# A recurrent attention and gated feed-forward kernel: the decay row on ScalarE's queue, more idle products in front, and a new order of emission

## The chip, the cores and the metric

The kernel runs on one core of one Trainium2 chip. The metric is the device time of one execution in microseconds (us), lower is better. The engines are named TensorE (PE, its weight loads PEld), VectorE (DVE), ScalarE (ACT), GpSimd (POOL) and SyncE (SP); an engine's instruction queue for DMA issues is written SPq or ACTq.

## The reference

An attention with a decaying state runs over 768 steps for 4 batches and 8 heads of width 48; its output feeds a layer with 3072 rows, 384 inputs and 2048 hidden units.

```python
def _attn_ref(r, k, v, w, u):
    state = np.zeros((B, H, D, D), dtype=np.float32)
    for t in range(S):
        kt, vt, rt = (k[:, :, t], v[:, :, t], r[:, :, t])
        cur = np.einsum('bhd,bhe->bhde', u[None] * kt, vt)
        y[:, :, t] = np.einsum('bhd,bhde->bhe', rt, state + cur)
        state = w[None, :, :, None] * state + np.einsum('bhd,bhe->bhde', kt, vt)

def _moe_ref(x, w_in, w_out):
    h = x @ w_in
    sp = np.where(h > 20.0, h, np.log1p(np.exp(np.minimum(h, 20.0))))
    return ((h * np.tanh(sp)) @ w_out).astype(np.float32)
```

## The kernel before

**Tiling.** The 768 steps are cut into 6 chunks of 128; a chunk and a batch make one attention step `s` (24 of them, `NS`). Four steps make one group of 512 rows, which then goes through the feed-forward layer in 16 tiles of hidden units (`up`: `hp` is a PSUM bank; `down`: three accumulators `acc0` to `acc2`). Each attention step has these pieces, each a small generator: `dots` (a product `q` of r and k on VectorE, and matrix products of it with `us`, two columns wide for the first two steps, whose sums `sd` ScalarE copies out), `scale` (multiplies r and k by powers of the decay, `TR`), `diag` (spreads `sd` over the diagonal of `P`), `keys` (multiplies k by the table `TKn`), `attend` (scores into `pa` or `pb`, and a predicated copy into `P`), `outputs` (rows of y into `yt` and `hp`, and the state), `finish` (copies y into `x`). Around them stand `convert` (weights arrive as 64-bit words and are turned to floats: one pass on ScalarE, three on VectorE), `split` (a weight into a high and a low part), and for each pair of tiles `evacuate` (copies `hp` to `hb`) and `gate` (two table loads, three functions on ScalarE, and on VectorE the product `gf` for the first tiles or `hb`, `gh` and `gl` for later ones).

**The first steps.** A prologue builds the powers of the decay from the decay row `wt`, a 2 KB transfer that SyncE issues ahead of everything else; VectorE's chain of L310 to L324 depends on it. SyncE then issues the list `FIRST` in order: `rk`, weight blocks (`raw`), `v`, `rkn`. ScalarE issues `cst`, the constants (mask, unit, `us`). `token_table` builds `TKn` from the decay powers: ScalarE spreads (L340), TensorE multiplies into `pb`, ScalarE copies (L351).

**Idle products.** `keep_warm` issues matrix products of zeros, which nothing reads. `WARM0` of them stand at the very front (three write into `pa` and `yt`, the rest into `idle`). Later, where the planner sees TensorE free for longer than `WARM_MIN`, it inserts `int(gap / FILL)` more; this ends with the first tile of the feed-forward layer.

```python
            if e == "pe" and self.fill and t - self.free[e] > WARM_MIN:
                begun = self.begun
                self.fill(t - self.free[e] - LAT)
...
    flow.fill = lambda us: keep_warm(int(us / FILL))
```

**The order.** The instructions of all engines are emitted in an order that a planner (`Flow`) computes when the kernel is built. It walks through the pieces, each a generator that yields what it waits for and what it costs on which engine, and picks at each turn the piece whose engine is free first, with a rank to break near ties. `RANK`, `CONVERT` and `SHIFT` move single pieces in rank; `FREE` tells when each engine is free at the start, `LAND0` and `LAND` when the first transfers land. `REST` is the order of the transfers after `FIRST`, issued one weight block at a time. On the chip each engine executes its own instructions in this order and waits on semaphores.

Of the kernel before, what the change touches and what calls it, by code (L numbers as in the profile page):

```python
# [76 lines left out]
def first_use(c):  # L77
    return UNITS.index((0, c) if c < AHEAD else (None, WG * c))
# [4 lines left out]
    ("rk", 3), ("v", 3), ("rkn", 1), ("rkn", 3), ("rkn", 0),  # L83
)
REST = (
    ("raw", 2), ("raw", 3), ("raw", 4), ("rk", 4), ("rkn", 4), ("v", 4), ("un", 0), ("raw", 6), ("raw", 5),
    ("raw", 7), ("raw", 8), ("raw", 9), ("raw", 10), ("raw", 12), ("raw", 13), ("raw", 11), ("raw", 14),
    ("raw", 15),
)
LAND0, LAND = 3.15, dict(rk=1.32, v=0.66, raw=1.96, rkn=0.5, un=0.78)  # L90
ISSUE, QUEUED, LANDING, USE, BACKLOG = 0.5, 0.95, 1.9, 0.6, 4.2
GATE = dict(raw3=1, raw4=2)
HT = 2 * C
# [2 lines left out]
BY_STEP = 0  # L96
FROM, FROM2 = 8, 14
X_SPLIT = 3
CONVERT = (-984.856, -938.676, -1001.12, -999.777)
LAG = 6  # L100
WHOLE = 0
AHEAD_LEAST, AHEAD_MOST, DOWN = 2, 8, 1
LO0, HI0, LO1, HI1 = 0.0, 0.7, 0.1, 0.9
LAT, LAT0 = 0.15, 0.13
WARM0, WARM_MIN, FILL = 10, 0.3, 0.28
DMA_LAT = 2.5
BLOCK0, BLOCK, ASK, HELD, FETCH = 445, 256, 0.7, 2.9, 2.5
PATIENCE = dict(dve=0.1, act=0.1, pe=0.3)
URGENT = 8
RANK = dict(token_table=-900.2, keys=-899.9, first_state=-899.5)  # L110

COST = dict(dve=1.0)
FREE = dict(pe=5.6, act=2.8, dve=1.0, pool=1.7, sp=1.0, landed=1.0)

L_ATT, L_V, L_IN, L_OUT, L_GATE, L_EVAC, L_PUT, L_FIN = 2, 2, 9, 9, 3, 1, 12, 4


SHIFT = dict(
    attend4=-8, attend6=8, attend7=3, convert10=30, convert15=-30, convert3=30, convert4=-30, convert7=1,
    convert8=-30, convert9=1, diag10=1, diag3=100, dots12=-1, dots6=100, dots8=30, evacuate12=-30, evacuate22=-30,  # L120
    evacuate6=-3, evacuate8=-3, gate0=-8, gate12=30, gate2=1, gate5=3, gate8=-30, keys11=3, keys3=-3, keys6=30,
    outputs5=-8, outputs6=1.742, outputs8=-8, outputs9=-8, scale11=-3, scale8=0.8, split1=8, split10=-30, split12=3,
    split9=-30,
)


# [128 lines left out]
def rwkv_mish_kernel(ctx, tc, rkT, rkN, vN, wT, w_in, w_out, consts, rkF, vF, wF, uF, outT):  # L255
    nc = tc.nc
# [9 lines left out]
    un = const.tile([128, DM], F32, name="un")  # L266
# [3 lines left out]
    wt, w64, iw = (small[:, 4 + n * NP : 4 + (n + 1) * NP] for n in range(3))  # L270
    flags = small[:, 4 + 3 * NP : 4 + 3 * NP + N_FLAGS]
    more = small[:, 4 + 3 * NP + N_FLAGS :]
    zeros = const.tile([128, 1], F32, name="zeros")
    nc.vector.memset(zeros, 0.0)
    nc.scalar.dma_start(cst, consts[:, : N_CST + 2 * NP])
    mask = cst[:, :CK].bitcast(U32)
    unit = cst[:, CK:N_CST].bitcast(BF16)
# [15 lines left out]
    order.enter_context(tc.manual_schedule(engines={ET.SP, ET.PE, ET.DVE, ET.Pool, ET.Activation}))  # L293
    loaded, loads = {}, {}
    sync = mybir.DependencyInfo(mybir.DependencyClass.Sync, mybir.DependencyReason.DATA)
    nc.sync.dma_start(wt, wT)


    powers = const.tile([128, NP, CK + 1], F32, name="TR")
# [5 lines left out]
    def prologue():  # L305

        yield "wt"
        v, M = nc.vector, CK // 2
        yield {"dve": 1.75}
        v.tensor_scalar(out=wc, in0=wt, scalar1=W_LO, scalar2=W_HI, op0=ALU.max, op1=ALU.min)  # L310
        n = 1
        while n < M:
            new, old = (powers[:, :, M + 1 + a : M + 1 + a + n] for a in (n, 0))
            v.tensor_tensor(
                out=new, in0=old, in1=powers[:, :, M + n : M + n + 1].broadcast_to([128, NP, n]), op=ALU.mult
            )
            n *= 2
        v.reciprocal(out=iw, in_=w32)
        v.tensor_tensor(
            out=powers[:, :, :M], in0=powers[:, :, M : 2 * M], in1=iw.unsqueeze(2).broadcast_to([128, NP, M]), op=ALU.mult  # L320
        )
        flow.set("TRK")
        yield {"dve": 0.1}
        v.tensor_tensor(out=w64, in0=w32, in1=w32, op=ALU.mult)  # L324
        flow.set("w64")
# [8 lines left out]
    def token_table():  # L334
        yield "w64"
        for par in range(2):
            r = ROWS[par]
            yield {"act": 0.65}
            for p in range(NP):
                nc.scalar.activation(dw[r, p, par], unit[r, : CK - 1 - D : -1], AF.Copy, scale=w64[r, p : p + 1])  # L340
        yield "x1"
        yield pe(0.9, 32)
        t = pb[1]
        for p in range(NP):
            for half in range(2):
                matmul(
                    t[HALVES[half], 2 * p * D : 2 * (p + 1) * D], lhsT=TR[:112, p],
                    rhs=dw[:112, p].rearrange("d q e -> d (q e)"), start=True, stop=True,
                )
        yield act(384)  # L350
        nc.scalar.copy(out=TKn, in_=t[:, :DM])  # L351
        flow.set("TKn")
# [39 lines left out]

    flow = Flow(FREE, 2 * WARM0)
    flow.events["wt"] = 2.6
# [283 lines left out]
    def keys(s):  # L678
        yield f"rkn{s}"
        yield f"sd{s}"  # L680
        yield "TKn"
        yield dve(384)
        k = loaded[s][1][:, :DM]
        nc.vector.tensor_tensor(out=k, in0=k, in1=TKn, op=ALU.mult)
        flow.set(f"keys{s}")
# [141 lines left out]
    def outputs(s):  # L827
# [32 lines left out]
        if not rows:  # L860
            flow.start(first_state(s), s + RANK["first_state"], name=f"first_state{s}")
        elif not last:
# [42 lines left out]
    def first_state(s):  # L905
        yield "out1"
        yield f"keys{s}"
        if s:
            yield f"state{s - 1}"
        yield pe(0.5, 64)  # L910
        state_products(s, new_first, True)
        for b in range(2):
            engine = yield {**act(192), **dve(192)}
            (nc.scalar.copy if engine == "act" else nc.vector.tensor_copy)(
                out=states[r112, 2 * s + b, :, :D], in_=new_first[b][r112]
            )
        flow.set(f"state{s}")
# [477 lines left out]
    for s in range(NS):  # L1395
        if s < 2:
            flow.start(spread_v(s), rank(s) + 0.0045, 0.0, f"spread_v{s}")
        for k, thread in enumerate((load_step, load_v, scale, dots, diag, keys, attend, outputs)):
            if thread is keys and s >= NS - 2 or s <= B and thread in (load_step, load_v):
                continue  # L1400
            if thread is keys and s < B:
                flow.start(keys(s), s + (RANK["keys"] if s < 2 else -899.8), 0.0, f"keys{s}")
                continue
# [6 lines left out]
    flow.start(prologue(), -1100, 0.0, "prologue")  # L1410
    flow.start(token_table(), RANK["token_table"], 0.0, "token_table")
    for c in range(len(W_ORDER)):
        i, f = W_ORDER[c]
        at = first_use(f) + (LAG - L_OUT if i else -L_IN) + c / 1000
        flow.start(convert(c), CONVERT[c] if c < len(CONVERT) else at, 0.0, f"convert{c}")
    for n, (i, f) in enumerate(S_ORDER):
# [13 lines left out]
    with tc.If(in_range < 128 * N_FLAGS):  # L1430
# [48 lines left out]
        with tc.tile_pool(name="any2", bufs=1) as work:  # L1479
            raw = work.tile([128, WE, 2], U32, name="raw")  # L1480
# [117 lines left out]
```

## Time and profile before

| | |
|---|---|
| median of 3 runs | 481.77 us (481.13 to 482.31) |
| span of the profiled execution | 479.8 us (its own time is not stated apart from the span) |
| PE busy | 469.6 us, 98% |
| DVE busy | 375.8 us, 78% |
| ACT busy | 385.7 us, 80% |
| DMA | 60.17 MB, mean 125 GB/s |

The busy time of TensorE counts idle products and products at a low clock as well. The shares of VectorE and ScalarE are means over the whole span; the first quarter and the rest differ.

### The profile page before, as it was taken

The numbers are of one execution on the slowest core, as the hardware profiler recorded it, in microseconds if no ns is written. First come the engines' busy times: TensorE is split into PE (matmuls) and PEld (weight loads), VectorE is DVE, ScalarE is ACT, GpSimd is POOL, SyncE is SP. The second block draws the span as 40 slices with busy tenths as digits, with TensorE's granted clock in tenths as the row PEclk, the third lists the DMA queues.
The fourth block names the chain that finished last, engine by engine and source line by source line (L and its number), as shares of the span: only waits on it lengthen the run. The fifth ranks groups of instructions, "written<-read, shape, count | busy, mean of one in ns | idle before, by whom it ended". The sixth has DMA issues, their size and how long they took to land.

```text
span 479.8 us, 11503 instructions
## 1 busy us (share of the span) xinstructions
PE 469.6 (98%) x4918; PEld 381.5 (80%) x4918; DVE 375.8 (78%) x599; ACT 385.7 (80%) x488; POOL 4.6 (1%) x31
## 2 busy tenths in 40 slices
PE   8989999999999999999999999999999999999995
PEld 5778988657887888888888888888888888888883
DVE  7997999998999794889875789987788745555650
ACT  5669799899989887667879877888569798989961
POOL 1000000000000000000000000000000000000000
PEclk8999999999999999999999999999999999999999
DMA  7866676430424210245132446143463220221002
GB/s 311 293 232 214 222 279 207 153 101 10 162 85 133 79 38 0 102 156 188 66 120 67 165 146 219 62 133 104 165 210 107 66 83 28 105 81 51 1 0 73
DMA packets 20171, 60.17 MB, mean 125 GB/s; under 512 B 3312, under 2 KB 4304, under 8 KB 20112
## 3 DMA queue, kind: packets, MB, share of 16 engines
q1 hardware_dynamic: 17664, 55.11, 34.1%
q10 hardware_dynamic: 2448, 4.25, 2.5%
q8 instruction: 40, 0.66, 0.6%
q14 instruction: 19, 0.16, 0.1%
HBM read 52.57 MB, written 4.72 MB: 119 GB/s over the span
## 4 chain that ended last, share of the span: by engine, by line
PE 90%; DVE 5%; ACT 2%; DMA 1%; issue 1%; ACTq 0%; SPq 0%
PE hp L358 41%; PE acc L358 41%; PE pa L358 4%; PE yt L358 2%; DVE w L499 1%; PE idle L358 1%; DMA rk<-in_rkT_dram 1%; DVE rk L606 1%; PE pb L358 1%; DVE gl L1054 1%; DVE hb L1046 1%; DVE hb L1222 0%; ACT w L497 0%; ACT L1036 0%; ACT L1030 0%
## 5 line engine op out<-in xcount | busy, mean ns | idle before, releaser
L358 PE MATMUL hp<-x,w 128*128 128x512 f32 x720 | 172.7, 392 | 0.9 <-DVE hb L1222 0.9
L358 PE MATMUL acc<-gh,w 128*128 128x512 f32 x492 | 158.5, 391 | 0.0
L358 PEld LDWEIGHTS hp<-x,w 128*128 128x128 f32 x720 | 134.2, 188 | 29.6 <-DVE hb L1222 1.0
L358 PEld LDWEIGHTS acc<-gh,w 128*128 128x128 f32 x492 | 92.3, 188 | 19.4
L358 PE MATMUL acc<-gl,w 128*128 128x512 f32 x246 | 95.1, 389 | 0.0
L1046 DVE TENSOR_TENSOR hb<-hb,fa 128x1024 f32<-128x1024 f32 x40 | 48.8, 1219 | 37.4 <-ACT fa L1036 37.3
L1030 ACT ACT_TABLE_LOAD x48 | 61.6, 1283 | 13.3 <-DVE hb L1046 9.8
L1036 ACT ACT_TABLE_LOAD x47 | 60.3, 1283 | 0.8
L1222 DVE COPY hb<-hp 128x512 f32<-128x512 f32 x63 | 43.2, 686 | 19.5 <-PE hp L358 19.2
L1030 ACT ACTIVATE fa<-hb,small 128x1024 f32<-128x1024 f32 x48 | 55.4, 1153 | 2.6 <-DVE hb L1046 2.1
L358 PEld LDWEIGHTS acc<-gl,w 128*128 128x128 f32 x246 | 46.2, 188 | 9.5
L1033 ACT ACTIVATE fa<-fa 128x1024 f32<-128x1024 f32 x48 | 50.9, 1059 | 0.8
L1036 ACT ACTIVATE fa<-fa 128x1024 f32<-128x1024 f32 x47 | 49.8, 1060 | 0.5
L1054 DVE TENSOR_TENSOR gl<-hb,gh 128x1024 fp32r<-128x1024 f32 x40 | 48.8, 1220 | 0.8 <-ACT gh L1050 0.2
L358 PE MATMUL acc<-gf,wraw 128*128 128x256 f32 (+1 forms) x132 | 37.7, 439 | 1.2 <-issue 1.2
L358 PEld LDWEIGHTS acc<-gf,wraw 128*128 128x128 f32 x132 | 25.6, 196 | 10.9 <-issue 8.6
L1222 ACT COPY hb<-hp 128x512 f32<-128x512 f32 x33 | 19.4, 587 | 17.5 <-PE hp L358 17.3
L606 DVE TENSOR_TENSOR rk<-rk,TR 112x1024 f32<-112x1024 f32 x22 | 26.8, 1218 | 0.1
L1050 DVE CAST gh<-hb 128x1024 fp32r<-128x1024 f32 x29 | 20.0, 690 | 7.0 <-PE acc L358 5.5
L358 PE MATMUL hp<-x,wraw 128*128 128x256 f32 x96 | 22.4, 386 | 0.0
L358 PEld LDWEIGHTS hp<-x,wraw 128*128 128x128 f32 x96 | 18.4, 196 | 2.0
L471 ACT ACTIVATE wraw<-wraw 128x768 f32<-128x768 uint32 x16 | 14.9, 930 | 6.3 <-DMA wraw<-in_w_out_dram 4.9
(143 smaller groups left out, 546.7 us busy)
## 6 DMA issues: line engine op xcount, KB each, us to landing
wraw<-in_w_in_dram SPq DMA_DIRECT2D x16, 768.0 KB, 4.6
wraw<-in_w_out_dram SPq DMA_DIRECT2D x16, 768.0 KB, 5.0
rk<-in_rkT_dram SPq DMA_DIRECT2D x22, 512.0 KB, 4.3
rkn<-in_rkN_dram SPq DMA_DIRECT2D x18, 384.0 KB, 4.9
v<-in_vN_dram SPq DMA_DIRECT2D x22, 256.0 KB, 4.4
out_dram<-ob ACTq DMA_DIRECT2D x10, 256.0 KB, 2.1
x<-x SPq DMA_DIRECT2D x60, 32.0 KB, 2.0
out_dram<-we ACTq DMA_DIRECT2D x6, 256.0 KB, 4.7
```

The costliest lines, as they stand in the source:

```text
L358: ins = nc.tensor.matmul(out, lhsT=lhsT, rhs=rhs, **flags)
L471: nc.scalar.activation(r, low, AF.Copy, bias=2.0, scale=2.0**-51)
L499: nc.vector.tensor_tensor(out=w[:, 1], in0=e, in1=w[:, 0].bitcast(F32), op=ALU.subtract)
L606: nc.vector.tensor_tensor(out=ab, in0=ab, in1=TR[:112].unsqueeze(1).broadcast_to([112, 4, NP, CK]), op=ALU.mult)
L1030: nc.scalar.activation(o.g, o.hb, AF.Sigmoid, bias=bias_ln2, scale=1.0)
L1033: nc.scalar.activation(o.g, o.g, AF.Arctan)
L1036: nc.scalar.activation(o.g, o.g, AF.Sin, scale=2.0)
L1046: nc.vector.tensor_tensor(out=o.hb, in0=o.hb, in1=o.g, op=ALU.mult)
L1050: (nc.scalar.copy if engine == "act" else nc.vector.tensor_copy)(out=o.gh, in_=o.hb)
L1054: nc.vector.tensor_tensor(out=o.gl, in0=o.hb, in1=o.gh.bitcast(F32), op=ALU.subtract)
L1222: (nc.scalar.copy if engine == "act" else nc.vector.tensor_copy)(out=o.hb[:, j], in_=h)
```

## The change

The load of the decay row moves from SyncE's queue, where it stood ahead of the list `FIRST`, to ScalarE's, ahead of `cst`. Thirteen idle products stand in front instead of ten, and gaps are filled at one per 0.24 us instead of 0.28. The planner's inputs (`REST`, `LAND0`, `CONVERT`, `RANK`, `FREE`, `SHIFT`) are new, and with them the order of emission on every engine.

```diff
 REST = (
-    ("raw", 2), ("raw", 3), ("raw", 4), ("rk", 4), ("rkn", 4), ("v", 4), ("un", 0), ("raw", 6), ("raw", 5),
-    ("raw", 7), ("raw", 8), ("raw", 9), ("raw", 10), ("raw", 12), ("raw", 13), ("raw", 11), ("raw", 14),
-    ("raw", 15),
+    ("raw", 2), ("raw", 3), ("raw", 4), ("rk", 4), ("v", 4), ("un", 0), ("rkn", 4), ("raw", 6), ("raw", 5), ("raw",
+    7), ("raw", 8), ("raw", 9), ("raw", 10), ("raw", 13), ("raw", 11), ("raw", 15), ("raw", 12), ("raw", 14),
 )
-LAND0, LAND = 3.15, dict(rk=1.32, v=0.66, raw=1.96, rkn=0.5, un=0.78)
+LAND0, LAND = 2.7, dict(rk=1.32, v=0.66, raw=1.96, rkn=0.5, un=0.78)
...
-CONVERT = (-984.856, -938.676, -1001.12, -999.777)
+CONVERT = (-765.0, -865.0, -1309.0, -995.0)
...
-WARM0, WARM_MIN, FILL = 10, 0.3, 0.28
+WARM0, WARM_MIN, FILL = 13, 0.3, 0.24
...
-RANK = dict(token_table=-900.2, keys=-899.9, first_state=-899.5)
+RANK = dict(token_table=-867.2, keys=-789.3, first_state=-1102.5)
...
-FREE = dict(pe=5.6, act=2.8, dve=1.0, pool=1.7, sp=1.0, landed=1.0)
+FREE = dict(pe=5.5, act=3.2, dve=1.0, pool=1.7, sp=1.0, landed=1.0)
...
 SHIFT = dict(
-    attend4=-8, attend6=8, attend7=3, convert10=30, convert15=-30, convert3=30, convert4=-30, convert7=1,
-    convert8=-30, convert9=1, diag10=1, diag3=100, dots12=-1, dots6=100, dots8=30, evacuate12=-30, evacuate22=-30,
-    evacuate6=-3, evacuate8=-3, gate0=-8, gate12=30, gate2=1, gate5=3, gate8=-30, keys11=3, keys3=-3, keys6=30,
-    outputs5=-8, outputs6=1.742, outputs8=-8, outputs9=-8, scale11=-3, scale8=0.8, split1=8, split10=-30, split12=3,
-    split9=-30,
+    attend4=41.0, attend7=84.0, convert8=-42.0, dots4=3.0, dots6=102.0, dots8=44.0, finish5=9.0, finish8=6.0,
+    gate2=83.0, gate8=-31.0, keys10=-25.0, outputs4=-39.0, outputs8=3.0, split3=18.0,
 )
...
+    nc.scalar.dma_start(wt, wT)
     nc.scalar.dma_start(cst, consts[:, : N_CST + 2 * NP])
...
-    nc.sync.dma_start(wt, wT)
```

## Rows read from the trace of the kernel before

**Rows 1.** The page: busy time by engine, and the chain by engine.

```profile
PE 469.6 (98%) x4918; PEld 381.5 (80%) x4918; DVE 375.8 (78%) x599; ACT 385.7 (80%) x488; POOL 4.6 (1%) x31
...
PE 90%; DVE 5%; ACT 2%; DMA 1%; issue 1%; ACTq 0%; SPq 0%
```

**Rows 2.** PE's waits: for what; us in total, times, longest.

```profile
PE acc L358 <- issue: 1.2, 1, 1.2
PE yt L358 <- DVE q L610: 1.1, 1, 1.1
...
PE hp L358 <- DVE hb L1222: 0.9, 1, 0.9
```

**Rows 3.** Windows: length, busy PE, PEld, DVE, ACT, POOL, PE clock, DMA share, GB/s.

```profile
5.00:41.00 36.00, 33.67 (x717) 27.27 (x718) 34.45 (x55) 24.61 (x54) 0.18 (x2) 0.91 0.75 271
41.00:113.00 72.00, 72.00 (x797) 55.95 (x797) 68.05 (x108) 64.88 (x99) 0.75 (x5) 1.00 0.57 189
...
147.00:474.00 327.00, 326.90 (x2893) 269.72 (x2893) 239.90 (x378) 262.45 (x298) 1.16 (x13) 1.00 0.30 98
```

**Rows 4.** Timeline of the first 5 us: start, length, instruction.

```profile
0.76 0.40 SPq L296 DMA_DIRECT2D small<-in_wT_dram  x1
0.77 0.41 ACTq L275 DMA_DIRECT2D cst<-in_consts_dram  x1
...
1.21 1.28 ACT L281 ACT_TABLE_LOAD   x1 [1.21 <-PEq L1585]
1.22 0.89 SPq L524 DMA_DIRECT2D rk<-in_rkT_dram  x2
...
2.20 2.62 PE L358 MATMUL idle<-zeros 128*128 128x512 bf16 x7
...
4.61 2.01 ACT L340 ACTIVATE pre<-cst,small 48x48 f32<-48x48 bf16 x8 [1.91 <-DVE small L324]
```

**Rows 5.** Timeline of VectorE, with idle time before and its releaser.

```profile
2.64 0.17 DVE L310 TENSOR_SCALAR TR<-small 128x4 f32<-128x4 f32 x1 [1.69 <-DMA small<-in_wT_dram]
...
4.37 0.16 DVE L324 TENSOR_TENSOR small<-TR 128x4 f32<-128x4 f32 x1
5.14 0.69 DVE L610 TENSOR_TENSOR q<-rk 112x512 f32<-112x512 f32 x1 [0.62 <-DMA rk<-in_rkT_dram]
...
19.78 1.03 DVE L684 TENSOR_TENSOR kn<-kn,TKn 128x384 f32<-128x384 f32 x2 [0.56 <-ACT TKn L351]
...
34.66 1.22 DVE L1044 TENSOR_TENSOR gf<-hb,fa 128x1024 f32<-128x1024 f32 x1
35.80 0.68 DVE L610 TENSOR_TENSOR q<-rk 112x512 f32<-112x512 f32 x1
36.52 1.23 DVE L606 TENSOR_TENSOR rk<-rk,TR 112x1024 f32<-112x1024 f32 x1
```

**Rows 6.** The chain that ended last, in the first 40 us.

```profile
1.22 3.90 DMA rk<-in_rkT_dram
...
9.81 0.88 PE idle L358 x2
...
13.03 2.51 PE idle L358 x8
...
16.39 0.54 PE idle L358 x2
...
34.76 1.22 issue
```

**Rows 7.** Windows: busy time and granted clock of three stretches.

```profile
4.11:7.52 3.41, 2.14 (x35) 1.44 (x37) 2.72 (x6) 2.17 (x9) 0.00 (x0) 1.00 1.02 413
7.52:10.94 3.42, 3.42 (x46) 2.46 (x40) 3.39 (x7) 2.13 (x7) 0.00 (x0) 0.50 1.07 419
...
33.00:36.40 3.40, 2.17 (x11) 1.67 (x10) 3.40 (x7) 1.08 (x2) 0.00 (x0) 1.00 0.65 245
```

## The prediction

> **What bounds the kernel now.** I read the page's busy shares and chain first. TensorE (PE) is busy for 469.6 of 479.8 us and the chain lies 90% on it [rows 1]: only time in which PE does nothing, or nothing useful, can be won. The list of PE's waits says where it does nothing: 1.1 us for VectorE's first product `q`, 1.2 us ahead of the first output product, 0.9 us for a copy of `hp` [rows 2]. The windows say where the others limit it. From 147 us on PE is busy for 326.90 of 327 us, so nothing gained or lost there but by PE's own work, which the change leaves alone. From 5 to 41 us VectorE (DVE) is busy for 34.45 of 36 us and from 41 to 113 us for 68.05 of 72, so over the first quarter two engines are nearly full at once [rows 3]. This matters most: what PE wins in front it keeps only if DVE also comes earlier.
>
> The profile's execution has a span of 479.8 us; the page states no other time of it. The median of the three runs is 481.77 us, 1.97 above, and I take that 1.97 as lying around the span and unchanged. 0.3% of 481.77 is 1.45 us, about what a measurement of this kernel can tell from no change: under 480.32 is faster, over 483.22 slower.
>
> **The load of the decay row.** SyncE issues `wt` at 0.76 us for 0.40 us, and so the first `rk` at 1.22. ScalarE issues `cst` at 0.77 [rows 4]. With `wt` on ScalarE's queue, `rk` goes out at about 0.76, that is 0.46 us earlier, and every load of FIRST behind it on that queue too. The decay row goes out at 0.77 instead of 0.76, so VectorE's chain on it still begins at 2.64 and ends at 4.37 + 0.16 = 4.53 [rows 5]. `rk` lands 3.90 us after its issue [rows 6], now at 4.66: the chain is out of the way by 0.13 us, and the first product `q` starts at 5.14 - 0.46 = 4.68. The cover is thin: were the decay row 0.3 us late on its new queue, 0.17 of the 0.46 would be gone. The gain is between 0 (if the transfers were bound by when the DMA engines wake, not by issue) and 0.46; the wait on that very transfer is a wait from its issue, so I take 0.46. Moved behind it, `cst` goes out at 1.2 instead of 0.77, and ScalarE's table load with it. ScalarE's next work that needs `cst` begins at 4.61 [rows 4], over 3 us later, and waits for VectorE anyway: cost nothing. Without that cover it would be 0.4.
>
> **Three more idle products in front.** The last of the seven that stand in one row ends at 2.20 + 2.62 = 4.82 [rows 4]; the first real product stands at 5.89, after a wait of 1.1 us [rows 2]. Two idle products took 0.88 us at the low clock, 0.44 each, and two took 0.54 at the full, 0.27 each [rows 6]. Three more are 0.81 at the full clock and end at 5.63, while the real product could now start at 5.89 - 0.46 = 5.43. So they fill the gap and run over by 0.2. That 0.2 lies beside VectorE's 0.69 us product and the rescale behind it, on which PE waits next, and I count it as nothing; were it not covered, 0.2 is the price.
>
> **Denser filling.** A gap that the planner sees is now divided by 0.24 instead of 0.28: 12 products stand in gaps in front (rows of 2, 8 and 2, of which three are shown [rows 6]), and 14 would. The two more cost between 2 x 0.27 = 0.54 and 2 x 0.44 = 0.88 where they run over a gap, nothing where they fit. What they may buy is the clock. From 4.11 to 7.52 PE was busy for 2.14 of 3.41 us, much of it with products two columns wide, and from 7.52 the granted clock was 0.50, the lower of the two levels (1.2 of 2.4 GHz). From 33.00 to 36.40 PE was busy for 2.17 us, but with wide products, and the clock stayed at 1.00 [rows 7]. With the gap in front filled, the first stretch holds about 1 us more of wide products, so I take it that the clock mostly stays. At the low clock the eight idle products at 13.03 took 2.51 us [rows 6]; at the full clock 8 x 0.27 = 2.16, and the dots and scores around them shrink also.
> The Trainium skill, "TensorE: Matmul & The Clock Gate", section "HAM oscillation — how this bites in real kernels", lets the clock fall only after a long spell of idleness. This trace disagrees: 1.27 of 3.41 us idle, in two pieces, was followed by the fall [rows 7]. By the page, filling small gaps would buy no clock, and the sum would be the one below without its second term.
>
> **What an earlier PE in front is worth.** VectorE starts the keys at 19.78 after an idle 0.56 us for `TKn`, which comes from PE's token table by way of ScalarE [rows 5]. If PE reaches that table at least 0.56 us sooner than VectorE, this idle time goes. PE's shrinkage (0.35 on the eight idle products, two late starts, and the dots and scores that ran at half clock) makes more than that: I take 0.56, with 0 at the other end. More than 0.46 + 0.56 = 1.02 us VectorE cannot come forward up to 35 us, in an unchanged order, since it has no other wait worth counting there.
>
> **The order of emission.** RANK, CONVERT, SHIFT and FREE feed one greedy planner, and a changed input reorders the instructions of all engines. No instruction of the real work is added or removed; what can change is stalls. The 1.22 us stall at 34.76 [rows 6] ends at 35.98, 0.1 us after the first `gf` on VectorE (34.66, 1.22 us [rows 5]): PE waits for the first gated product and has nothing else in its queue. In the old order this stall grows by what PE gains and VectorE doesn't. A new order can give PE other work there, or the gate an earlier place: between all 1.22 gained and, below, a loss (the slower rival). I take half, 0.6, since an order computed from better start times will see this gap but VectorE is full there. The 0.9 us stall at 146 [rows 2] is between 0 and 0.88 gained, and a new order may leave one of its size: I take 0. The reordered REST moves only weight blocks against each other and one key load behind `un`; with VectorE idle for 72 - 68.05 = 3.95 us in 41 to 113 [rows 3], a block a few us late is hidden there, and PE had no wait on one.
>
> **Sum.** 0.46 + 0.56 + 0.6 = 1.62 us off the span: 478.2, and off the median: 481.77 - 1.62 = 480.15 us.
>
> **The rivals.**
> *All of it comes (faster by more).* Both stalls vanish and VectorE's two gains come: 0.46 + 0.56 + 1.22 + 0.88 = 3.12, so 478.65 us; if the order also saves PE the front time that VectorE's 1.5 us of idle time in 5 to 41 leaves open, about 478. For it: PE is nearly all of the span. Against: full VectorE.
> *VectorE holds it (no change).* PE comes sooner, waits longer at 34.76, and only the earlier load counts, or not even that: between 481.77 - 0.46 = 481.3 and 481.77. For it: VectorE's 34.45 of 36 us.
> *The clock falls all the same.* Then the second term goes and the denser filling costs up to 0.88 on PE: -0.46 - 0.6 + 0.88 = -0.18, so 481.6 us; for it, that the dots stay two columns wide. If instead the front rises to full clock later than at 4.11 in some run, the three products cost 3 x 0.44 = 1.32 and end at 6.14, 0.7 after the real product could start, with the same result within 0.3.
> *The new order starves PE (slower).* The old SHIFT held `gate0` 8 places forward, and the new one doesn't. Behind the first `gf` on VectorE stand step 4's product and rescale, 0.68 and 1.23 us [rows 5]. Put ahead of it, they delay the first output products by 1.91 us; with the same at one more gate in the stretch to 113 us, where VectorE also is full, 3.82 - 0.46 - 0.56 = +2.8, so 484.6 us. It decides the sign from the point where such delays exceed 1.02 + 1.45 = 2.47 us in all, that is, with the second gate. Against it: the planner sees these costs.
>
> **How the numbers follow.** Forecast 0.40, all of it 0.20, VectorE holds 0.14, the clock falls 0.10, starved 0.16. The predicted time is the forecast's, 480.15 us. Its own range is 479.2 to 481.2, as the 0.6 goes from 0 to 1.22 and the 0.56 to 0; 0.26 of its 0.40 lies under 480.32. So faster 0.26 + 0.20 = 0.46; same 0.14 + 0.14 + 0.10 = 0.38; slower 0.16. For eight in ten the range leaves out the ends: below 478.0 (a part of the 0.20) and above 483.0 (most of the 0.16).
>
> **What would show it.** After the change: the first `rk` issued at about 0.76 and `q` at 4.7 (the first term); PE without a wait before its first dots; granted clock 1.00 from 7.5 to 14 us (else the clock rival); keys without the wait for `TKn`, 1 us earlier (the second term); the wait ahead of the first `acc` under 1.2 us (the third) or longer (VectorE holds, or starved, by how long). From 147 us on PE should stay without waits. The prediction is wrong if PE's waits in 30 to 147 us add up to over 3 us, or if the useful products begin no earlier.

## The result, and the profile after

The changed kernel is slower: a median of 484.95 us (4 runs, 484.73 to 485.16) against 482.04 us for the kernel before on the same chip (4 runs, 481.13 to 482.53). The ratio is 1.006, with a 95% interval of 1.0044 to 1.0075. The profiled execution took 484.73 us, and its span is 482.9 us, so 1.83 us lie around the span, where I had taken 1.97.

Busy time and the chain, from the page (in the order of [rows 1]):

```profile
PE 473.8 (98%) x4923; PEld 383.3 (79%) x4923; DVE 373.0 (77%) x593; ACT 389.0 (81%) x503; POOL 4.4 (1%) x31
...
PE 91%; DVE 4%; ACT 2%; DMA 1%; issue 0%; ACTq 0%
```

The chain still lies on PE, for 91%. PE is busy for 4.2 us longer, and its idle time fell from 479.8 - 469.6 = 10.2 to 482.9 - 473.8 = 9.1 us. So the loss does not show as waiting; idle products and time at the low clock count as busy.

So I look at when fixed pieces of real work begin. Four such marks of the kernel before, from its timeline: the first and the second tile of the feed-forward layer, the first output products, and the last copy to the output (start, length, instruction).

```profile
18.81 2.87 PE L358 MATMUL hp<-x,wraw 128*128 128x256 f32 x12
...
23.42 2.86 PE L358 MATMUL hp<-x,wraw 128*128 128x256 f32 x12
...
35.98 2.83 PE L358 MATMUL acc<-gf,wraw 128*128 128x256 f32 x12 [1.23 <-issue]
...
473.94 0.59 ACT L1076 COPY we<-acc 128x512 f32<-128x512 f32 x1 [0.74 <-PE acc L358]
```

The same kind of rows after, with the first 10 us ahead of them (these answer to [rows 4] and [rows 5]):

```profile
0.76 0.87 SPq L520 DMA_DIRECT2D rk<-in_rkT_dram  x2
0.76 0.41 ACTq L271 DMA_DIRECT2D small<-in_wT_dram  x1
...
2.20 4.34 PE L354 MATMUL idle<-zeros 128*128 128x512 bf16 x10
...
4.61 0.17 DVE L306 TENSOR_SCALAR TR<-small 128x4 f32<-128x4 f32 x1 [3.65 <-DMA small<-in_wT_dram]
...
6.33 0.16 DVE L320 TENSOR_TENSOR small<-TR 128x4 f32<-128x4 f32 x1
6.41 0.69 DVE L606 TENSOR_TENSOR q<-rk 112x512 f32<-112x512 f32 x1
...
7.15 1.05 PE L354 MATMUL yt<-cst,q 112*128 112x2 f32 x8 [0.60 <-DVE q L606]
...
20.57 2.87 PE L354 MATMUL hp<-x,wraw 128*128 128x256 f32 x12
...
25.18 2.87 PE L354 MATMUL hp<-x,wraw 128*128 128x256 f32 x12
```

`rk` is issued at 0.76, as forecast. But the decay row, issued in that very moment on the other queue, lets VectorE's chain begin only at 4.61 instead of 2.64, after 3.65 us of waiting for that transfer. The chain's last operation ends at 6.49; `q`, whose `rk` is there by then but which stands behind the chain in VectorE's order, starts at 6.41, where 5.14 stood before and 4.68 was forecast. The first dots follow at 7.15, the first tile at 20.57 instead of 18.81, the second at 25.18 instead of 23.42: both 1.76 us later.

The list of transfers (size, median us from issue to landing) says it in one line each. Before:

```profile
small<-in_wT_dram SPq DMA_DIRECT2D x1, 2.0 KB, 1.9
```

After:

```profile
small<-in_wT_dram ACTq DMA_DIRECT2D x1, 2.0 KB, 3.8
```

The later marks, from the timeline of after:

```profile
36.20 0.68 DVE L606 TENSOR_TENSOR q<-rk 112x512 f32<-112x512 f32 x1
...
37.03 0.64 PE L354 MATMUL pa<-cst,q 48*64 48x1 f32 x32 [0.53 <-DVE q L606]
37.06 1.22 DVE L602 TENSOR_TENSOR rk<-rk,TR 112x1024 f32<-112x1024 f32 x1
...
38.20 1.22 DVE L1040 TENSOR_TENSOR gf<-hb,fa 128x1024 f32<-128x1024 f32 x1
...
39.52 4.52 PE L354 MATMUL acc<-gf,wraw 128*128 128x256 f32 x12 [0.49 <-PE pa L354]
...
477.64 0.58 ACT L1072 COPY we<-acc 128x512 f32<-128x512 f32 x1 [0.74 <-PE acc L354]
```

Step 4's product `q` and its rescale now stand ahead of the first `gf` on VectorE; before they stood behind it [rows 5]. PE meanwhile does step 4's sums and scores into `pa`, with a wait ahead of the sums (0.53 us), ahead of the scores (0.67) and behind them (0.49). The first output products begin 3.54 us later than before (39.52 against 35.98), and take 4.52 us instead of 2.83. The last copy begins 3.70 us later; the span is 3.1 us longer, since what follows the start of that copy took 479.8 - 473.94 = 5.86 us before and 482.9 - 477.64 = 5.26 after.

PE's waits after (us in total, times, longest; they answer to [rows 2]):

```profile
PE pa L354 <- DVE rk L602: 1.2, 3, 0.7
...
PE yt L354 <- DVE q L606: 0.6, 1, 0.6
PE pa L354 <- DVE q L606: 0.5, 1, 0.5
PE acc L354 <- PE pa L354: 0.5, 1, 0.5
```

Both long waits of [rows 2], 1.2 us ahead of `acc` and 0.9 us for `hb`, are gone. And the windows (columns as in [rows 3]):

```profile
5.00:41.00 36.00, 33.52 (x712) 25.32 (x711) 32.87 (x56) 24.85 (x61) 0.18 (x2) 0.90 0.71 255
41.00:113.00 72.00, 72.00 (x797) 57.08 (x796) 66.16 (x106) 64.61 (x98) 0.40 (x5) 0.98 0.57 195
147.00:474.00 327.00, 326.65 (x3011) 269.58 (x3011) 244.66 (x384) 265.49 (x299) 1.40 (x14) 1.00 0.30 99
6.14:9.55 3.41, 2.60 (x47) 2.01 (x45) 3.38 (x7) 2.91 (x10) 0.00 (x0) 1.00 1.02 408
9.55:16.38 6.83, 6.83 (x95) 4.08 (x95) 6.62 (x11) 3.84 (x14) 0.00 (x0) 0.51 1.04 396
40.27:43.69 3.42, 3.42 (x10) 2.74 (x9) 2.04 (x3) 3.41 (x8) 0.00 (x0) 0.52 0.80 274
```

From 147 us on PE is busy for 326.65 of 327 us, next to the 326.90 of before, as forecast. The last three rows show the clock: its first recorded change, to the full level, is at 6.14 us; it was granted in full for 3.41 us, then stood at half level until 16.38, and fell once more at 40.27 for 3.42 us, under the first output products.

### The profile page after: what moved, and what is told of

The parts are those of the page before. It is cut to its first block, busy times and chain, and to the rows that moved or that the text cites. A ratio compares the mean times of both kernels' runs of the same rounds, so it can differ in the third digit from the quotient of the medians.

```text
span 482.9 us, 11529 instructions
## 1 busy us (share of the span) xinstructions
PE 473.8 (98%) x4923; PEld 383.3 (79%) x4923; DVE 373.0 (77%) x593; ACT 389.0 (81%) x503; POOL 4.4 (1%) x31
## 4 chain that ended last, share of the span: by engine, by line
PE 91%; DVE 4%; ACT 2%; DMA 1%; issue 0%; ACTq 0%
PE hp L354 42%; PE acc L354 41%; PE pa L354 4%; PE yt L354 2%; PE idle L354 1%; DVE rk L602 1%; DMA small<-in_wT_dram 1%; PE pb L354 1%; ACT L1032 1%; DVE hb L1042 1%; ACT fa L1032 0%; DVE w L495 0%; DVE hb L1218 0%; ACT L1026 0%; DVE q L606 0%
## 5 line engine op out<-in xcount | busy, mean ns | idle before, releaser
L1026 ACT ACT_TABLE_LOAD x48 | 61.6, 1283 | 15.0 <-DVE hb L1042 12.5
L354 PE MATMUL acc<-gf,wraw 128*128 128x256 f32 (+1 forms) x132 | 39.5, 455 | 0.5 <-PE pa L354 0.5
L354 PEld LDWEIGHTS acc<-gf,wraw 128*128 128x128 f32 x132 | 26.6, 204 | 9.8 <-issue 6.3
L354 PE MATMUL hp<-xp,w 128*128 128x512 f32 x72 | 18.7, 408 | 0.0
```

Of the source, the lines that this page charges most:

```text
L354: ins = nc.tensor.matmul(out, lhsT=lhsT, rhs=rhs, **flags)
L1026: nc.scalar.activation(o.g, o.hb, AF.Sigmoid, bias=bias_ln2, scale=1.0)
```

## The experiments

Ratios are to the kernel before on the same chip, with 95% intervals. Kernels that keep one order but issue other idle products tell the planner the old number (`planned`), so that the rest of the order stays the same; the two lines of `keep_warm` that this takes are shown once, with the order alone. `...` marks lines left out.

### The decay row

**The changed kernel with the row back on SyncE, ahead of `rk`.**

```diff
-    nc.scalar.dma_start(wt, wT)
     nc.scalar.dma_start(cst, consts[:, : N_CST + 2 * NP])
...
+    nc.sync.dma_start(wt, wT)
```

> The changed kernel with the decay row back on SyncE's queue ahead of the first rows; order of emission and idle products as in the change. Theory (the row's small transfer shares the DMA engines with the first 512 KB of rk, issued in the same moment, and so landed 3.8 instead of 1.9 us after its issue): the row lands by 2.7 us, VectorE's chain begins 1.9 us earlier, the first product q at about 5.1, and the time falls by 1.3 to 2 us, to 483 to 483.7. Rival (the late row costs nothing in the end, since the order of emission sets the stalls after 30 us): the row is early, but the time stays at 484.5 to 485.2.

Measured: 482.61 us over 12 runs, ratio 1.0014 (0.9997 to 1.0031). The row landed in 1.8 us, the chain began at 2.62 and `q` at 4.99. One moved line is worth 484.95 - 482.61 = 2.34 us (0.46% or 2.2 us by the two ratios), more than I had expected of it, and most of the loss. The marks:

```profile
16.72 0.69 DVE L606 TENSOR_TENSOR q<-first 112x512 f32<-112x512 f32 x1 [0.91 <-DMA first<-in_rkT_dram]
...
18.15 2.87 PE L354 MATMUL hp<-x,wraw 128*128 128x256 f32 x12
...
23.39 2.86 PE L354 MATMUL hp<-x,wraw 128*128 128x256 f32 x12
```

The first tile begins at 18.15, 2.42 us earlier than in the changed kernel, but the second only 1.79 earlier, at 23.39, where it stood before. VectorE waits until 16.72 for the `rk` of step 3 to land. This bears on the second term of the sum, below.

**The kernel before with only the row moved** to ScalarE's queue, ahead of `cst`.

```diff
+    nc.scalar.dma_start(wt, wT)
     nc.scalar.dma_start(cst, consts[:, : N_CST + 2 * NP])
...
-    nc.sync.dma_start(wt, wT)
```

> The kernel before with one line moved: the decay row on ScalarE's queue ahead of cst; order of emission and idle products unchanged. Theory: the row lands at about 4.6 us, q starts at 6.4 instead of 5.1, and the time rises by 1.3 to 2 us to 483.3 to 484. By the prediction it would fall by 0.46. Rival: the row is late but is made up for before 40 us, so no change (482.0 within 0.5).

Measured: 483.78 us over 6 runs, ratio 1.0038 (1.0026 to 1.0051). The row landed 4.2 us after its issue, the chain began at 5.04, PE waited 2.2 us for `q`, the first tile began at 21.32 (in this execution the clock was first recorded to rise at 16.4 us, so that mark is not the row's alone). Alone, the first edit of the change costs 0.38% of 482.24 = 1.8 us.

Two theories were left for why it lands late: ScalarE's queue is slow, or the row has lost its start ahead of `rk`, whose packets it then shares the DMA engines with. The next two kernels tell them apart.

**The changed kernel with a head start**: the row stays first on ScalarE's queue, and `cst` moves to SyncE ahead of `rk`, so that `rk` leaves later.

```diff
-    nc.scalar.dma_start(cst, consts[:, : N_CST + 2 * NP])
...
+    nc.sync.dma_start(cst, consts[:, : N_CST + 2 * NP])
```

> The changed kernel with cst issued on SyncE ahead of rk, so that rk leaves about 0.46 us after the decay row, which stays on ScalarE's queue. Theory (a shared start is the cause): the row lands by about 2.8 us and the time is that of the row back on SyncE, 483 to 483.7. Rival (ScalarE's queue itself is slow with its first transfer): the row lands at 4.5 or later and the time stays near 485.

Measured: the row landed in 2.1 us on the same queue, as this timeline shows:

```profile
0.77 0.41 ACTq L271 DMA_DIRECT2D small<-in_wT_dram  x1
...
1.21 0.89 SPq L520 DMA_DIRECT2D rk<-in_rkT_dram  x2
...
2.86 0.17 DVE L306 TENSOR_SCALAR TR<-small 128x4 f32<-128x4 f32 x1 [1.91 <-DMA small<-in_wT_dram]
```

With 0.44 us between the two issues the chain begins at 2.86. So ScalarE's queue is not slow. The time, 483.65 us over 12 runs (1.0033, 1.0017 to 1.0049), came back by 1.3 us, less than with the row on SyncE. In its profiled execution the clock stood at half level under the first tile (3.88 us for twelve products instead of 2.87), and `q` started at 5.47, 0.48 later than with the row on SyncE. Whether that explains the other 1.0 us was not tested, and the two intervals overlap.

**The kernel before with the row on its own old queue, but behind the first `rk`.**

```diff
-    nc.sync.dma_start(wt, wT)
...
+                if s == 0:
+                    nc.sync.dma_start(wt, wT)
```

> The kernel before with the decay row on SyncE's queue behind the first 512 KB of rk instead of ahead of it; all else unchanged. Theory (the row is late because rk's bytes are on the same DMA engines ahead of it, whichever queue): the row's landing is 3.5 to 4.5 us after its issue, VectorE's chain begins after 4.5 us, and the time is 1.3 to 2 us over the kernel before (483.5 to 484.2). Rival (two queues that start at the same moment hinder each other, one queue doesn't): the row lands 1.9 to 2.4 us after its issue, by 3.6, and the time is within 0.6 of the kernel before.

Measured: 484.01 us over 10 runs, ratio 1.0036 (1.002 to 1.0051), and the row again 3.8 us from issue to landing:

```profile
0.76 0.40 SPq L524 DMA_DIRECT2D rk<-in_rkT_dram  x1
...
1.21 0.42 SPq L526 DMA_DIRECT2D small<-in_wT_dram  x1
...
5.00 0.17 DVE L310 TENSOR_SCALAR TR<-small 128x4 f32<-128x4 f32 x1 [4.05 <-DMA small<-in_wT_dram]
```

On SyncE or on ScalarE, a row issued with or behind the first 512 KB takes 3.8 to 4.2 us; with 0.44 us or more of lead it takes 1.8 to 2.1. The lead decides, and not the queue. The Trainium skill, "DMA: Bandwidth & Descriptors", section "Issuing engines are not separate DMA queues", states what fits this: transfers that several engines issue run on the same 16 DMA engines and interleave, and a second queue saves only the time of issuing. The 3.8 us on either queue agree with it.

### The order of emission

**The new order alone**: all of the planner's new inputs, but the row on SyncE ahead of `rk` and the old number of idle products (ten in front, gaps filled at one per 0.28 us).

```diff
-    nc.scalar.dma_start(wt, wT)
...
+    nc.sync.dma_start(wt, wT)
...
-    def keep_warm(n, out=None):
+    def keep_warm(n, out=None, planned=0):
...
-            flow.begun += 2 * n
+            flow.begun += 2 * planned
...
-    keep_warm(WARM0 - 3)
+    keep_warm(10 - 3)
...
-    flow.fill = lambda us: keep_warm(int(us / FILL))
+    flow.fill = lambda us: keep_warm(int(us / 0.28), planned=int(us / FILL))
```

> The new order of emission alone: decay row on SyncE's queue, ten idle products in front and gaps filled at one per 0.28 us as before, every engine otherwise in the change's order. If the order is neutral: 482.0 to 482.6, no change. By the prediction's third term it would be 0.6 faster, 481.6. By the starved rival (step 4's product and rescale stand ahead of the first gated product on VectorE): first output product at 37.5 us or later instead of 36.0, and 483.5 or more.

Measured: 483.3 us over 12 runs, ratio 1.002 (1.0003 to 1.0037). The new order costs about 1.0 us where I had booked a gain of 0.6. Two other comparisons give less: the kernel with the row back on SyncE, which has the new idle products too, lies 0.14% or 0.7 us over the kernel before, with an interval that holds 1, and with the late row and the old idle products the new order (1.0051, below) lies 0.13% or 0.6 us over the old one (1.0038, above). From the second tile to the last copy its profile has 476.19 - 24.71 = 451.48 us, against 473.94 - 23.42 = 450.52 before: 0.96 us. The window between these marks, here and in the kernel before:

```profile
24.71:476.19 451.48, 449.06 (x4508) 367.22 (x4500) 354.10 (x556) 373.91 (x461) 2.15 (x23) 1.00 0.36 116
...
23.42:473.94 450.52, 448.36 (x4508) 366.97 (x4500) 356.61 (x562) 371.06 (x446) 2.35 (x23) 1.00 0.35 116
```

PE is idle for 2.42 us in the first and for 2.16 in the second. So waits account for 0.26 of the 0.96 us; 0.70 lies in time that counts as busy, at the full clock in both. The two other profiles of this order with an early row have 451.67 (back on SyncE) and 451.36 us (head start) between these marks. Seven of the nine of the old order have 450.48 to 450.89, but the two with thirteen idle products in front and one per 0.45 us, below, have 451.80 and 451.32: single profiles scatter by about as much as the order costs.

**The first gate forward**, on the kernel with the row back on SyncE: the old order held it 8 places forward, and the new doesn't.

```diff
-    gate2=83.0, gate8=-31.0, keys10=-25.0, outputs4=-39.0, outputs8=3.0, split3=18.0,
+    gate0=-40.0, gate2=83.0, gate8=-31.0, keys10=-25.0, outputs4=-39.0, outputs8=3.0, split3=18.0,
```

> The row back on SyncE's queue, with the change's idle products and inputs of the planner, and the first gate put 40 places forward in rank, so that step 4's rescale stands behind the first gated product on VectorE (the planner then also moves later instructions). If that rescale ahead of the gate costs what it takes: 1.2 us faster than with the row alone moved back (482.6), about 481.4. If the scores that wait on the rescale fill the same stall on TensorE: within 0.5 of 482.6.

Measured: 488.43 us over 6 runs, ratio 1.013 (1.0098 to 1.0162), a miss. The planner moved much of what follows as well. PE's waits in it:

```profile
PE acc L354 <- issue: 2.5, 1, 2.5
PE hp L354 <- DVE x L949: 1.6, 2, 1.3
PE pa L354 <- issue: 1.3, 1, 1.3
```

The wait ahead of `acc`, which the new order had done away with, is back and twice as long. So either the place of the gate in the new order is not what it costs, or this remedy costs more; the run doesn't tell which.

**The stall around step 4's scores filled**: six idle products, two ahead of each half and two behind, to see whether the second fall of the clock at 40.27 makes the loss. First with the row on SyncE, then with it on ScalarE.

```diff
-    def keep_warm(n, out=None):
+    def keep_warm(n, out=None, planned=None):
...
-            flow.begun += 2 * n
+            flow.begun += 2 * (n if planned is None else planned)
...
     def scores(s):
         rk = loaded[s][0]
+        if s == B: keep_warm(2, planned=0)
         if with_sums(s):
...
+        if s == B: keep_warm(2, planned=0)
         for p in range(NP):
...
+        if s == B: keep_warm(2, planned=0)
         flow.set(f"scores{s}")
```

> The changed kernel with the row back on SyncE's queue, and six more idle products of 0.22 us in TensorE's waits around step 4's scores (two ahead of the sums, two ahead of the scores, two behind), ahead of the first output product. If the second stretch at the low clock near 40 us is what the new order costs: no execution with a mean clock of 0.989 or less, and 481.8 to 482.2 us instead of 482.6. If longer stalls are the cost: 482.4 to 483.

> The changed kernel as it is (late row) with the same six idle products. If the second low stretch costs it what its trace shows (3.4 us at half clock): granted clock 1.00 from 34 us on and 1 to 1.7 us faster than 484.95, 483.2 to 484. If stalls alone set it: 484.6 to 485.2.

Measured: 483.38 us over 12 runs, ratio 1.0022 (1.0009 to 1.0035), and 485.11 us over 6 runs, ratio 1.0063 (1.0044 to 1.0082): neither is faster than its pair without them, 482.61 and 484.95. With the row on SyncE no execution has a mean clock under 0.991, where four of the twelve without the filling had 0.987 to 0.989; the time is still not the 481.8 to 482.2 us of the theory. So with an early row the second fall is not what the order costs, unless the six products cost as much as the clock gives back, which this run can't separate. With the late row the clock did stay up in the profiled execution:

```profile
36.00:41.00 5.00, 4.66 (x78) 3.55 (x80) 4.32 (x6) 3.24 (x4) 0.00 (x0) 1.00 0.33 91
41.00:45.00 4.00, 4.00 (x21) 3.63 (x20) 1.93 (x4) 3.99 (x9) 0.00 (x0) 1.00 0.91 332
```

But that execution is the fastest of the six, 483.56 us at a mean clock of 0.996; the other five stand at 0.986 to 0.992, so their median does not tell what the fall costs. The profiles tell more. These are the windows from the second tile to the last copy in the two of the new order whose clock fell near 40 us (the changed kernel, and the one with the old idle products, below); over so long a window the mean clock still rounds to 1.00:

```profile
25.18:477.64 452.46, 450.40 (x4507) 368.53 (x4500) 353.94 (x556) 374.57 (x461) 2.15 (x23) 1.00 0.35 116
...
26.04:478.53 452.49, 450.41 (x4508) 368.38 (x4500) 354.05 (x556) 374.80 (x462) 2.19 (x23) 1.00 0.35 116
```

They are 0.8 to 1.1 us longer than the 451.36 to 451.67 of the three without a fall and without filling; the output products alone took 4.52 - 2.83 = 1.69 us more. With the stall filled and the late row the same window has 452.31 us: the six products seem to have taken about what the clock gave back. So in its profile the fall is a part of the changed kernel's loss, beside the row and the order; how much of the median it makes is not shown.

### The idle products

**The kernel before with the new number of them** (thirteen in front, one per 0.24 us of gap) in the old order.

```diff
-    keep_warm(WARM0 - 3)
+    keep_warm(13 - 3)
...
-    flow.fill = lambda us: keep_warm(int(us / FILL))
+    flow.fill = lambda us: keep_warm(int(us / 0.24), planned=int(us / FILL))
```

> The kernel before with the change's idle products alone: thirteen in front and gaps filled at one per 0.24 us, five more in all, in the very places of the old order. Theory (where the clock falls the fillings run over their gaps at 0.43 us each): the clock falls all the same, the first tile of the feed-forward layer starts 0.5 to 0.9 us later, and the time rises by 0.4 to 1 us, to 482.4 to 483. By the prediction (the clock stays up): the granted clock is 1.00 from 7.5 to 14 us and the time falls by about 0.5.

Measured: 481.92 us over 12 runs, ratio 0.9998 (0.9982 to 1.0015). Nothing that can be told was gained or lost; the interval leaves room for 0.9 us less and 0.7 us more. The windows on both sides of the clock's fall:

```profile
4.55:7.97 3.42, 3.21 (x48) 2.19 (x46) 3.00 (x5) 2.17 (x9) 0.00 (x0) 1.00 0.98 391
7.97:14.87 6.90, 6.90 (x96) 4.25 (x96) 5.99 (x11) 4.18 (x14) 0.00 (x0) 0.52 1.03 408
```

PE was busy for 3.21 of 3.42 us, where the kernel before had 2.14 [rows 7], and the clock fell all the same.

**Fewer of them**: the kernel before with gaps filled at one per 0.45 us, 7 instead of 12.

```diff
-    flow.fill = lambda us: keep_warm(int(us / FILL))
+    flow.fill = lambda us: keep_warm(int(us / 0.45), planned=int(us / FILL))
```

> The kernel before with its gaps filled at one idle product per 0.45 us: five fewer, seven instead of twelve, in the places and order of before. If the filling that runs over its gap at the low clock sets the first tile's start: the second row (eight products, now five) ends up to 1.3 us sooner, the first tile starts by 18 us instead of 18.9, and the time falls by 0.3 to 1 us. If VectorE holds the rest, or the clock is low for longer with fewer of them: 481.7 to 482.7, no change.

Measured: 481.95 us over 12 runs, ratio 0.9999 (0.9985 to 1.0013). The first tile came 0.36 us earlier, at 18.45, and the second at 23.34.

**Thirteen in front, and gaps at one per 0.45**, in the kernel before.

```diff
-    keep_warm(WARM0 - 3)
+    keep_warm(13 - 3)
...
-    flow.fill = lambda us: keep_warm(int(us / FILL))
+    flow.fill = lambda us: keep_warm(int(us / 0.45), planned=int(us / FILL))
```

> A version that may beat both: the kernel before, in its order, with thirteen idle products in front (the clock then rose early in each of the five profiles that had thirteen) and gaps filled at one per 0.45 us (seven products instead of twelve). If the first tile's start sets the end: first tile by 18 us, and the time 0.5 to 1 us under the kernel before, 481.1 to 481.6. If rk of step 3, which landed at 16.5 to 16.7 us in each run with an early front, sets the second tile: first tile early, second tile still at 23.2 to 23.4 us, and the time within 0.4 of 482.1.

Measured: 482.32 us over 12 runs, ratio 1.0011 (0.9996 to 1.0026). No gain either.

**The changed kernel with the old idle products**, row on ScalarE: does the late row need them?

```diff
-    keep_warm(WARM0 - 3)
+    keep_warm(10 - 3)
...
-    flow.fill = lambda us: keep_warm(int(us / FILL))
+    flow.fill = lambda us: keep_warm(int(us / 0.28), planned=int(us / FILL))
```

> The changed kernel with the late row and the new order but with ten idle products in front and gaps filled at one per 0.28 us. If the idle products do nothing, as in the old order: 484.7 to 485.3. If their filling over the gaps costs here: 0.4 to 0.9 us faster, 484.0 to 484.5. If they hold the clock up: slower than 485.3.

Measured: 485.12 us over 6 runs, ratio 1.0051 (1.0034 to 1.0068), the same as with them. PE now waited 2.9 us for `q` instead of 0.6, and it made no difference to the time.

### What holds the front when PE comes earlier

**Less work on VectorE**: the kernel before without the rescale of steps 2 and 3, 2 x 1.22 us. This leaves out part of the computation: the scores of these two steps are not scaled.

```diff
-        nc.vector.tensor_tensor(out=ab, in0=ab, in1=TR[:112].unsqueeze(1).broadcast_to([112, 4, NP, CK]), op=ALU.mult)
+        if s not in (2, 3): nc.vector.tensor_tensor(out=ab, in0=ab, in1=TR[:112].unsqueeze(1).broadcast_to([112, 4, NP, CK]), op=ALU.mult)
```

> The kernel before, leaving out VectorE's rescale of steps 2 and 3 (two operations of 1.22 us each at 14 and 17 us), so that these two steps' scores are those of unscaled rows; order otherwise unchanged. If VectorE holds the stretch to 36 us: the first gated product comes up to 2.4 us earlier, TensorE's 1.2 us wait for it goes, and the time falls by 1 to 2.4 us, to 479.7 to 481.1. If TensorE's front holds it (prediction's second term): the wait shrinks by under 0.5 and the time stays within 0.5 of 482.1.

Measured: 481.67 us over 12 runs, ratio 0.9988 (0.9972 to 1.0004). At most 0.28% of 482.05 = 1.35 us came of 2.44 us less work, and perhaps none. In its profile VectorE stood idle instead:

```profile
21.40 1.03 DVE L684 TENSOR_TENSOR kn<-kn,TKn 128x384 f32<-128x384 f32 x2 [3.02 <-ACT TKn L351]
```

Part of this wait may be the clock's: in this execution it was first recorded to rise at 16.6 us, against 4.11 before.

**The keys of steps 2 and 3 on GpSimd**, in the kernel before.

```diff
-        nc.vector.tensor_tensor(out=k, in0=k, in1=TKn, op=ALU.mult)
+        (nc.gpsimd if s in (2, 3) else nc.vector).tensor_tensor(out=k, in0=k, in1=TKn, op=ALU.mult)
```

> A version that may beat both: the kernel before with the two key products of steps 2 and 3 (0.53 us each on VectorE) on GpSimd, which is idle there. If VectorE holds the stretch to 36 us: the first gated product comes about 1 us earlier and the time falls by 0.5 to 1 us, to 481.1 to 481.6. If GpSimd is slow and the states wait for it, or VectorE slows while GpSimd works: 482.1 or more.

Measured: 482.26 us over 12 runs, ratio 1.0 (0.9981 to 1.0019). The first tile began at 17.82, the earliest of all, but the second at 23.18, and `q` of step 3 waited until 16.51 for its `rk`. The first `gf` began at 34.79, against 34.66 before: taking 1.06 us of work off VectorE did not bring it forward.

**The `rk` of step 3 exchanged with the weight block ahead of it in `FIRST`** (on the kernel with thirteen in front and one per 0.45).

```diff
-        for what, s in FIRST:
+        for what, s in [{("raw", 1): ("rk", 3), ("rk", 3): ("raw", 1)}.get(x, x) for x in FIRST]:
```

> The same with the transfers of rk of step 3 and of the second weight block exchanged on SyncE's queue, so that rk of step 3 goes first; all instructions otherwise in the same order. If the landing of rk of step 3 sets the second tile: VectorE's product of step 3 starts by 15.9 instead of 16.6 us, the second tile comes 0.5 to 1 us earlier (by 22.8), and the time falls by as much against the same kernel without the exchange. If the weight block is as late as rk was: second tile at 23.2 to 23.6 and no change; if it is much later, slower by up to 1.3 us.

Measured: 482.79 us over 12 runs, ratio 1.0013 (0.9997 to 1.0028), a miss. Now it is the weight block that lands at 16.55, with ScalarE waiting 4.56 us for it (idle before its pass over that block). The first tile began at 18.00 and the second at 24.30; but the first took 4.55 us instead of 2.87, most of it at the low clock, so this late second tile is no measure of the loads. Whichever of the two is put last lands at about 16.5 us.

## Why the prediction was wrong, point by point

**The step that failed** is the first term, "The load of the decay row": "The decay row goes out at 0.77 instead of 0.76, so VectorE's chain on it still begins at 2.64". It took the 1.69 us that VectorE waited for the row as a property of that transfer, when it was one of its lead over `rk`: without the lead the row landed 3.8 us after its issue instead of 1.9. Half of the term came as written (`rk` leaves at 0.76), and that is what spoiled the other half. In place of `q` 0.46 us earlier came `q` 1.27 us later, and in place of -0.46 us a loss of 1.7 to 2.3 us of the 2.9 measured: 1.8 from the row alone on the old kernel, 0.36% of 482.05 = 1.7 for the row behind `rk`, 2.34 between the changed kernel and its pair. The text called the cover thin and priced a row 0.3 us late; it was 2 us late. No rival held this case. With the row early the changed kernel stands at 482.61, inside the range up to 483.0; with it late the old order alone stands at 483.78.

**Moving `cst`** cost nothing, as said: ScalarE's table work waited for VectorE's chain, to 6.58 instead of 4.61.

**Three more idle products** were right at nothing, for another reason. With the late row they ended at 2.20 + 4.34 = 6.54, ahead of the dots at 7.15; and without them PE waits longer for the same `q`.

**Denser filling and the second term (-0.56).** Filling made PE busier ahead of 7.97 us and did not keep the clock up: the rival "The clock falls all the same" had this right. The Trainium skill, "TensorE: Matmul & The Clock Gate", section "HAM oscillation — how this bites in real kernels", gives the same outcome for another reason: it ties the fall to a long idle spell, and by it there should have been no fall to prevent, with 3.42 - 3.21 = 0.21 us idle ahead of it. The measurement decides, against that rule and against my own step, which took it that the clock mostly stays once the gap in front is filled. One price in that step was also misread: of the eight idle products at 13.03, taken as at the low clock, more than half ran at the full one, since the clock of the kernel before rose again at 14.35; at 0.44 us each, eight take 3.5 us and not 2.51. An earlier PE would probably not have paid either. The kernels whose first tile came at 17.8 to 18.5 us (the new order with the row on SyncE, fewer idle products, keys on GpSimd) all began the second at 23.2 to 23.4, as before, and in all three profiles `q` of step 3 waits for its `rk` until 16.5 to 16.7. I read this as the loads of the first 17 us, together, setting a floor there. The DMA share, 0.98 to 1.04 in the windows shown from 4.55 to 16.38 us, and the 16.5 us at which the exchanged weight block landed agree with that. The floor is not a fixed time, though: in the kernel before and in the new order alone, whose fronts were later, `q` of step 3 began at 15.67 and 15.82 without a wait. A kernel with fewer bytes in front was not run, so it is not shown outright. The keys' wait for `TKn` that the term wanted to remove, 0.56 us, was 1.10 in the changed kernel. The row alone does not set it: there was none with the late row and the stall filled, and 1.70 with the row early in the new order alone, whose clock rose only at 16.3.

**The order (-0.6)** had the wrong sign. The stall of 1.2 us did get other work, as hoped, and the 0.9 us stall went too. Yet the new order by itself costs about 1.0 us (1.002, 1.0003 to 1.0037), or 0.6 to 0.7 by the other two comparisons, and PE's idle time after the second tile is no shorter (2.42 us against 2.16): what left those two places came back in smaller waits. Where the rest goes, 0.70 us of busy time in that profile, is open. The second fall of the clock is not needed for it, since three profiles of the order without that fall are 0.8 to 1.2 us behind the kernel before all the same; in the changed kernel it comes on top. Moving the gate forward made it worse.

**The slower rival** gave 484.6 us, close to the 484.95, but by another mechanism. Step 4's `q` and rescale did go ahead of the first `gf`, as it says, and delay the first output products; PE does step 4's scores in that time, and need not do them later. The order accounts for 0.6 to 1.0 us and not for 2.8.

**VectorE holds it** found no support: 1.06 and 2.44 us less work on VectorE moved the time by nothing that these intervals can tell, though up to 1.35 of the 2.44 us is not excluded.

**The sum as measured**: the row +1.7 to 2.3, the order +0.6 to 1.0, the idle products 0, in all 2.3 to 3.3, against 484.95 - 482.04 = 2.91 us. The second fall of the clock stands in no term of its own; where it came, it lies in these. The test written down in advance for a failure, PE's waits in 30 to 147 us over 3 us, did not strike (PE is idle for 1.7 us there); the other, useful products that begin no earlier, did.

No version here beats both kernels: the two lowest medians that do the whole work, 481.92 and 481.95, can't be told from the kernel before.

## What to carry to other kernels

A small transfer from which a long chain starts needs a lead over the bulk loads, on whichever queue it is issued (here 0.44 us was enough); read its landing in the list of transfers and ask what is issued in the same half microsecond, before moving it or what follows it. Follow a gain in front to the next piece that joins other inputs (here the second tile and its loads) before putting it into the sum. Stalls that a new order removes must be added up against those it makes, over the whole span, and an order's worth is measured alone.

## What the runs showed of the hardware

- A 2 KB transfer issued in the same moment as 512 KB on another queue, or 0.45 us behind it on the same one, landed after 3.8 to 4.2 us; with 0.44 us of lead after 2.1, and ahead of it on one queue after 1.8 to 1.9.
- When the granted clock rises and falls in front differs from execution to execution. With ten idle products in front, the first recorded change of the clock, to the full level, is at 16.3 to 16.7 us in four of the eight profiles and at 3.7 to 5.7 in the other four. Ahead of that change the views print 1.00, but the pace of the products is that of the low level: with only the row moved and with only the new order, two idle products at 10 to 12.5 us still took 1.01 us. With thirteen the rise came at 3.7 to 7.3 us in all nine profiles. The medians of the kernel before with thirteen and with ten were still the same, so one profile's clock says little about a kernel's time.
- GpSimd took 4.33 us for two 128x384 products that take VectorE 0.53 to 0.55 us each, and one operation of VectorE that ran beside them took 1.65 us instead of 0.96; others beside them, such as the two key products of 0.55 us each, were not slowed:

```profile
18.83 4.33 POOL L684 TENSOR_TENSOR kn<-kn,TKn 128x384 f32<-128x384 f32 x2 [16.06 <-DMA wraw<-in_w_in_dram]
...
22.33 1.65 DVE L478 SCALAR_TENSOR_TENSOR we<-wraw,we 128x768 uint32<-128x768 uint32 x1
```
